# A hash-attention and feed-forward kernel rebuilt around units of 256 queries

## The chip, the cores and the metric

The kernel runs on one core of one Trainium2 chip. Times are device microseconds (us) of that core. The execution that the profiler recorded has a span from the first to the last instruction; the time of a run is a little longer than its span. A "ratio" below is the mean time of one kernel's fast runs over the mean time of the other's fast runs of the same rounds, so it is not the ratio of the medians that stand beside it. A run counts as fast within 1.5% of the fastest run of its kernel in the same rounds; the kernel before varies more than that, so ratios of different rounds are not comparable with one another, and kernels are compared below by their medians. PE is the matmul engine, PEld its weight loads, DVE the vector engine, ACT the engine for exp, POOL the general one, SP the one that issues most DMAs. "The clock" is the granted PE clock that the profile lists, 1.00 being full speed. PSUM is the memory in which the kernels keep the outputs of their matmuls; a bank is here a piece of it of 512 fp32 columns. A row group is one of the four sets of 32 partitions (32i to 32i+31).

## The reference

Four batches, eight heads, 768 positions, head size 64. A query attends to the keys that have the same six-bit hash; the result is normalised over 512 features and goes through a feed-forward of 512 to 2048 to 512 with a residual.

```python
q_bits = (np.einsum('bhsd,dk->bhsk', q, proj) > 0)        # 6 bits; k_bits the same
mask = q_bucket[:, :, :, None] == k_bucket[:, :, None, :]  # bucket: the 6 bits as a number
scores = np.where(mask, q @ k.T / sqrt(64), -1e9)
attn = softmax(scores)                                     # its sum gets + 1e-9
x = (attn @ v), heads side by side -> [4, 768, 512]
xn = (x - mean) / sqrt(var + 1e-6) * g_ln
out = x + maximum(xn @ w_ch1, 0) @ w_ch2
```

Both kernels get the mask from a matmul: the six signs of q and k are extra rows of the contraction, so that a pair with unequal signs gets a score so low that exp makes it nothing.

## The kernel before

For each batch three stages follow one another: a prologue (transposes, hashes), attention, and normalisation with feed-forward.

```python
for b in range(B):
    ...
    for h in range(H):                       # prologue: transposes in fp32
        ...
                        nc.tensor.transpose(tp[:, c, :], src[:, hh * half + c, :], identf)
                    nc.vector.tensor_copy(dstf[:, sl], tp)      # fp32 copy, for the hash
                    nc.scalar.copy(dst[:D, sl], tp)             # bf16 copy, for the scores
    for srcf, dst, mul in ((qTf_b, qprime_b, BIG), (kTf_b, kprime_b, 1.0)):
        for hx in range(HS // 512):          # prologue: hashes, fp32, 6 output rows
            ...
            nc.tensor.matmul(sp, proj_f, srcf[:, sl])
            nc.scalar.sign(dpart, sp)
    for h in range(H):                       # attention
        for qg in range(n_qg):
            for kj in range(n_stile):
                nc.tensor.matmul(sc, kprime[:, ksl], rhs_q)     # 70 rows: 64 and 6 signs
                nc.scalar.activation(expb, sc, AF.Exp, scale=scale, bias=bias_sb)   # 384 columns
                nc.tensor.matmul(avp, v_aug[:, kj, :], expb, ...)   # v is stationary
            ...                              # copy, PE transposes back, division
    ...                                      # normalisation, PE transposes
    for nt in range(n_htile):                # feed-forward, first half; then the second
        ...
```

The softmax here doesn't subtract the row's maximum and nothing guards it: scores larger than these inputs give would overflow.

## Time and profile before

The median was 741.25 us over the first three runs (723.31 to 741.81). In all later rounds this kernel gave times between 713 and 743 us; the shorter runs are those with a higher mean clock (712.96 us at 0.885, 741.52 us at 0.827 in the same rounds); why the clock differs was not examined. The profiled run is one of the short ones, with a span of 714.1 us at clock 0.878.

From the chain of waits in order of time:

| stage, by batch | where in the span (us) | what is busy |
|---|---|---|
| loads and weight casts | 0 to 31 | DMA |
| prologue | 31 to 108, and 60 us in each later batch | PE, on fp32 |
| attention | about 52 us in each batch | ACT |
| normalisation and feed-forward | about 54 us in each batch | PE, on bf16 |

The page of the kernel before, busy tenths in 40 slices of 17.9 us, by engine, with the granted clock under them:

```profile
PE   0089999978997998996997798996998898997897
ACT  0044439974206437994303536995312543997420
PEclk9999999998999556997999855997999755898899
```

ACT is at 9 only where attention runs. PE is near 9 nearly everywhere, but in each of the three later batches the clock falls to 5 or 6 for two or three slices. The table of windows for one piece of attention, one of feed-forward and one of the hashes shows what these are (columns: window; its length; busy us and instruction count of PE, PEld, DVE, ACT, POOL; clock; share of DMA; GB/s):

```profile
110.00:120.00 10.00, 9.80 (x52) 4.93 (x51) 5.28 (x28) 9.88 (x22) 0.00 (x0) 1.00 0.00 0
200.00:215.00 15.00, 13.77 (x64) 5.97 (x64) 3.97 (x7) 1.18 (x3) 0.00 (x0) 1.00 0.27 98
255.00:275.00 20.00, 18.87 (x25) 2.69 (x24) 0.00 (x0) 6.96 (x12) 0.00 (x0) 0.50 0.03 6
```

Attention: ACT is busy for 9.88 of 10 us. Feed-forward: PE alone works, at full clock. Hashes: PE alone works, 18.87 of 20 us, at half clock. The groups of instructions of the same run (line, engine, operation, output and inputs with their shapes, count, then busy us and the mean ns of one, then idle time before them):

```profile
L152 ACT ACTIVATE expb<-sc,bias_sb 128x384 bf16<-128x384 f32 x384 | 182.9, 858 | 0.6
L153 PE MATMUL avp<-expb,vaug_b 128*65 128x384 bf16 x384 | 129.3, 337 | 10.3 <-ACT expb L152 9.0
L133 PE MATMUL spf<-kTf_b,proj_f 64*6 64x512 f32 x96 | 84.0, 1051 | 0.0
L133 PE MATMUL spf<-qTf_b,proj_f 64*6 64x512 f32 x96 | 69.9, 819 | 1.5 <-DVE qTf_b L125 1.5
L206 PE MATMUL hp<-xnT,w_sb 128*128 128x384 bf16 x512 | 94.7, 330 | 3.6 <-ACT xnT L198 3.4
```

The hashes keep PE busy for 84.0 + 69.9 = 154 us to produce 6 rows. Such a line's busy time counts overlapping instructions once, so 384 exps in 182.9 us are 0.476 us each, although one takes 858 ns from start to end.

### The profile page before, as it was taken

How to read it: one execution, taken by the hardware profiler on the slowest of the kernel's cores; microseconds unless marked ns; L12 is line 12 of the kernel's file. 1: busy time of each engine (PE TensorE's matmuls, PEld its weight loads, DVE VectorE, ACT ScalarE, POOL GpSimd, SP SyncE). 2: the span in 40 equal slices, each digit the busy share in tenths (PEclk: the TensorE clock that was granted, in tenths of full speed). 3: DMA queues.
4: the chain of work that ended last, by engine and by line, in shares of the span. 5: the costliest groups of instructions: out<-in, count | busy, mean ns of one | idle time of the engine just before them, and what ended most of it. 6: DMA issues, size and time to landing. Idle time of an engine off the chain costs nothing.

```text
span 714.1 us, 7683 instructions
## 1 busy us (share of the span) xinstructions
PE 611.2 (86%) x2520; PEld 242.2 (34%) x2528; DVE 307.8 (43%) x1028; ACT 359.5 (50%) x728; POOL 19.0 (3%) x44
## 2 busy tenths in 40 slices
PE   0089999978997998996997798996998898997897
PEld 0022214435542212443542212443543221443553
DVE  0444304676325402668424510668423420568431
ACT  0044439974206437994303536995312543997420
POOL 0010000010000000002000000002000000000000
PEclk9999999998999556997999855997999755898899
DMA  8674300012023200003013310002013200000001
GB/s 316 210 135 99 73 17 1 0 42 49 10 82 96 67 11 0 1 2 88 12 59 89 85 23 0 1 2 55 13 45 88 56 1 0 1 2 0 1 15 74
DMA packets 81576, 34.32 MB, mean 48 GB/s; under 512 B 75776, under 2 KB 75776, under 8 KB 81024
## 3 DMA queue, kind: packets, MB, share of 16 engines
q1 hardware_dynamic: 81536, 33.83, 17.7%
q8 instruction: 20, 0.33, 0.2%
q14 instruction: 20, 0.16, 0.1%
HBM read 27.53 MB, written 6.29 MB: 47 GB/s over the span
## 4 chain that ended last, share of the span: by engine, by line
PE 79%; DVE 8%; ACT 7%; DMA 4%; issue 1%; SPq 0%
PE spf L133 21%; PE hp L206 13%; PE avp L153 12%; PE sc L150 10%; PE tp L121 7%; DMA w_f<-in_moe_w_ch_dram 3%; PE avt_p L162 3%; ACT qprime_b L135 2%; ACT kprime_b L126 2%; DVE stats L178 2%; PE xnTp L195 2%; DVE qTf_b L125 1%; DVE xn L191 1%; ACT qprime_b L126 1%; ACT xnT L198 1%
## 5 line engine op out<-in xcount | busy, mean ns | idle before, releaser
L152 ACT ACTIVATE expb<-sc,bias_sb 128x384 bf16<-128x384 f32 x384 | 182.9, 858 | 0.6
L153 PE MATMUL avp<-expb,vaug_b 128*65 128x384 bf16 x384 | 129.3, 337 | 10.3 <-ACT expb L152 9.0
L150 PE MATMUL sc<-qprime_b,kprime_b 70*128 70x384 bf16 x384 | 130.6, 347 | 0.0
L206 PE MATMUL hp<-xnT,w_sb 128*128 128x384 bf16 x512 | 94.7, 330 | 3.6 <-ACT xnT L198 3.4
L158 DVE CAST avs<-avp 65x384 bf16<-65x384 f32 x64 | 35.4, 552 | 130.8 <-PE avp L153 130.8
L135 ACT ACTIVATE qprime_b<-spf 6x512 bf16<-6x512 f32 x48 | 28.2, 588 | 123.9 <-PE spf L133 123.9
L121 PE MATMUL tp<-identf,qnat 128*64 128x128 f32 x192 | 40.4, 343 | 52.7 <-DMA qnat<-in_q_dram 34.5
L133 PE MATMUL spf<-kTf_b,proj_f 64*6 64x512 f32 x96 | 84.0, 1051 | 0.0
L133 PE MATMUL spf<-qTf_b,proj_f 64*6 64x512 f32 x96 | 69.9, 819 | 1.5 <-DVE qTf_b L125 1.5
L125 DVE COPY kTf_b<-tp 64x384 f32<-64x384 f32 x64 | 35.1, 549 | 79.2 <-PE tp L121 79.1
L206 PEld LDWEIGHTS <-w_sb 128*128 128x128 bf16 x512 | 50.0, 98 | 43.1 <-issue 10.7
L211 ACT ACTIVATE hbuf<-hp 128x384 bf16<-128x384 f32 x64 | 31.4, 490 | 57.2 <-PE hp L206 57.2
L213 DVE TENSOR_SCALAR hbuf<-hp 128x384 bf16<-128x384 f32 x64 | 35.7, 558 | 53.4 <-PE hp L206 51.3
L153 PEld LDWEIGHTS <-vaug_b 128*65 128x65 bf16 x384 | 44.2, 116 | 39.2 <-issue 24.4
L150 PEld LDWEIGHTS <-kprime_b 70*128 70x128 bf16 x384 | 38.5, 101 | 55.7 <-issue 46.6
L135 ACT ACTIVATE kprime_b<-spf 6x512 bf16<-6x512 f32 x48 | 28.2, 588 | 56.1 <-PE spf L133 56.1
L218 PEld LDWEIGHTS <-hbuf 128*128 128x128 bf16 x384 | 37.5, 98 | 44.8
L121 PE MATMUL tp<-identf,knat 128*64 128x128 f32 x192 | 44.9, 347 | 7.1 <-ACT qprime_b L126 7.1
L166 DVE CAST avt<-avt_p 128x65 f32<-128x65 bf16 x192 | 37.5, 223 | 22.6 <-PE avt_p L162 17.9
L126 ACT CAST qprime_b<-tp 64x384 bf16<-64x384 f32 x64 | 30.1, 472 | 31.0 <-DVE qTf_b L125 30.6
L121 PEld LDWEIGHTS tp<-identf,knat 128*64 128x64 f32 x192 | 20.0, 131 | 73.3 <-issue 43.2
L125 DVE COPY qTf_b<-tp 64x384 f32<-64x384 f32 x64 | 34.2, 547 | 24.3 <-PE tp L121 24.0
(152 smaller groups left out, 447.6 us busy)
## 6 DMA issues: line engine op xcount, KB each, us to landing
w_f<-in_moe_w_ch_dram SPq DMA_DIRECT2D x2, 4096.0 KB, 19.6
qnat<-in_q_dram SPq DMA_DIRECT2D x32, 192.0 KB, 2.5
knat<-in_k_dram SPq DMA_DIRECT2D x32, 192.0 KB, 2.6
vnat_f<-in_v_dram SPq DMA_DIRECT2D x32, 192.0 KB, 2.9
out_dram<-res SPq DMA_DIRECT2D x24, 256.0 KB, 2.0
gln_sb<-in_moe_g_ln_dram SPq DMA_DIRECT2D x1, 256.0 KB, 4.9
proj_f<-in_proj_dram SPq DMA_DIRECT2D x1, 1.5 KB, 1.9
```

What stands on the lines that cost most here:

```text
L121: nc.tensor.transpose(tp[:, c, :], src[:, hh * half + c, :], identf)
L125: nc.vector.tensor_copy(dstf[:, sl], tp)
L126: nc.scalar.copy(dst[:D, sl], tp)
L133: nc.tensor.matmul(sp, proj_f, srcf[:, sl])
L135: nc.scalar.sign(dpart, sp)
L150: nc.tensor.matmul(sc, kprime[:, ksl], rhs_q)
L152: nc.scalar.activation(expb, sc, AF.Exp, scale=scale, bias=bias_sb)
L153: nc.tensor.matmul(avp, v_aug[:, kj, :], expb, start=(kj == 0), stop=(kj == n_stile - 1),)
L166: nc.vector.tensor_copy(avt, avt_p)
L206: nc.tensor.matmul(hp, w1_sb[:, dt, nt * P : (nt + 1) * P], xnT[:, dt, msl], start=(dt == 0), stop=(dt == n_dtile - 1),)
L213: nc.vector.tensor_scalar_max(hbuf[:, nt, msl], hp, 0.0)
L218: nc.tensor.matmul(o2, hbuf[:, nt, si * P : (si + 1) * P], w2_sb[:, nt, :], start=(nt == 0), stop=(nt == n_htile - 1),)
```

## The change

The kernel is written anew, with a schedule by hand: every piece of work gets a key, a step number, and all pieces are issued in the order of their keys. A unit is 256 queries of all eight heads, and takes six steps; a step treats four heads, two key tiles and 256 queries. The intent: fewer and wider instructions, PE transposes removed, and feed-forward of earlier units issued between the steps of later ones, so that PE always has work while ACT does the exps. The core of the new kernel (cuts marked):

```diff
-            for kj in range(n_stile):
-                nc.tensor.matmul(sc, kprime[:, ksl], rhs_q)
-                nc.scalar.activation(expb, sc, AF.Exp, scale=scale, bias=bias_sb)
-                nc.tensor.matmul(avp, v_aug[:, kj, :], expb, ...)
+    def scores(s):                       # 24 matmuls; head i uses rows 32i to 32i+31, bank i
+        sc[s] = psum.tile([P, 4, 512], F32, name=f"sc{s}", tag="sc")     # one buffer, 4 banks
+        for kk in range(2):
+            for rep in range(3):         # 6 sign rows, then two halves of 32 features
+                for i in range(4):
+                    r = slice(32 * i, 32 * i + (NB if rep == 0 else 32))
+                    ...
+                    nc.tensor.matmul(sc[s][:, i, 256 * kk : 256 * kk + 256], lh, rh, ...)
+    def exps(s):                         # one instruction of 2048 columns
+        nc.scalar.activation(E[s], sc[s], AF.Exp, scale=EXP_SCALE, bias=bias_sb)
+    def av(s):                           # exp is stationary, v streams: 16 matmuls of 65 columns
+        for kk in range(2):
+            for i in range(4):
+                for qt in range(2):
+                    nc.tensor.matmul(acc[u, g][:, qt, (D + 1) * i : (D + 1) * (i + 1)],
+                        E[s][:, i, 256 * kk + P * qt : ...], vaug[u // 3][:, 4 * g + i, 2 * kp + kk], ...)
 ...
+    def turn(dst, src, j, kj0, n):       # q and k: 32x32 transposes on DVE
+        nc.vector.transpose(d[:, j, kj0 : kj0 + n], s[:, j, kj0 : kj0 + n])
+    def flip(u):                         # normalised rows: transposes by DMA
+        nc.sync.dma_start_transpose(out=xnT[u][:, qt], in_=xc[u][:, qt])
 ...
+    def ff1(u, p, bank):                 # a chunk: 8 matmuls of 256 columns, then a relu
+        f1 = psum.tile([P, 2, 256], F32, name=f"f1_{u}{p}", tag=bank)    # one bank
+        ...
+        nc.vector.tensor_scalar_max(hb[u][:, 2 * p : 2 * p + 2], f1, 0.0)
+    def ff2(u, t, qtr, bank):            # a chunk: 4 matmuls of 512 columns
 ...
+    for s in range(NS):                  # 72 steps
+        at(s, scores, s)
+        at(s + 0.05, exps, s)
+        at(s + 1.07, av, s)
+    def ff(fn, *a):                      # the feed-forward chunks, 2.67 in a step, from step 8.5 on
+        key = 8.5 + 0.375 * chunk[0]
+        chunk[0] += 1
+        at(key, fn, *a)
```

Hashes of the first batch are small fp32 matmuls at the start; those of later batches use four column groups of 32, during the steps of the batch before, and 16 small DMAs bring their bits to the right rows. The casts of q, k and v are POOL's, the layer norm's scale is folded into the first weight, and `vsum` with a factor of 2^-100 gives rows without any matching key the mean of v that the reference gives them.

## The prediction

> **What bounds the kernel now.** Stage by stage (table of windows, chain of waits), the kernel does three things for each of four batches, almost one after the other: a prologue of fp32 transposes and fp32 hash matmuls (about 77, 60, 58 and 61 us), attention (about 52 us each) and layer norm with feed-forward (about 54 us each), after 31 us of weight loads and casts. Each stage has another limit. The prologue is bound by PE: in the groups of instructions the hash matmuls (64x512 fp32, only 6 output rows) are busy for 154 us and are 21% of the chain; the fp32 transposes are busy for 85 us. While the hash matmuls run alone the granted clock falls to 0.50. Attention is bound by ACT: in the timeline an exp of 128x384 starts every 0.47 us, with ACT 100% busy and PE waiting. Feed-forward is bound by PE[...]: 16 matmuls of 384 columns take 2.74 us (171 ns each), 16 of 512 take 3.45 us (216 ns each), while ACT and DVE are mostly idle.
>
> **What the change does.** It puts the three stages on top of each other, so that the sum of three limits becomes about the PE's sum. Removed from PE: the transposes of q and k (to DVE's 32x32 transposes), of the attention output (exp is now stationary, so queries come out on partitions) and of the normalised rows (to DMA). Hashes become 12 small full-width matmul pairs in batch 0 and six column-tiled groups after. Exps become 72 of 2048 columns.
>
> **Cost, per step (72 steps).**
> - ACT: the measured 0.47 us for 384 columns[...].
> - PE scores: 24 row-tiled matmuls of 256 columns.[...]
> - PE values: 16 pairs of a 128-column weight load and 65 streamed columns[...].
> - PE feed-forward: the same 393k columns; 2.67 chunks of 0.86 to 0.96 us: 2.43.
> - Fallback rows and hashes[...]
> Sum 4.9 us. Scores have a single PSUM buffer, so exp, scores, exp is a serial chain of about 3.4 us; it is hidden under 4.9 us and binds only in the first 8.5 steps, which have no feed-forward.
>
> **Total.** Start about 10, 8.5 steps at 3.5 (30), 63.5 steps at 4.9 (310), a tail of 26 chunks (24), last store 4: span about 378; times were somewhat above the span before (714 against 723 to 742), so about 387 us.
>
> **What would show it.** PE over 90% busy with clock near 1.0 from about 40 us on; no fp32 transposes on PE; step period (start to start of exps) 4.9 us in the middle, 3.5 at the beginning; ACT about 35 to 40%; DVE about 40 to 45%; ff matmuls at 110 to 125 and 216 ns; a PE-only tail of 20 to 27 us.
>
> **What would make it wrong.** Row tiles that do not overlap (scores 2.6 us a step: +100 us).[...] The single banks of the feed-forward: relu from PSUM (0.56 us for 384 columns now, so about 0.7 for 512) behind other DVE work could stall PE.[...] Slower than before would need the serial chain above 9 us a step.

The sum of a step came to 4.9 us. Of its terms only feed-forward still stands, with 2.43 us, the author's estimate from the 216 ns and 171 ns measured for 512 and 384 columns. The other 2.5 us are the cut terms for scores with changes of tiling, for values, and for fallback rows and hashes. The chain of about 3.4 us, and with it the 3.5 us of the first steps, has cut terms in it too, for exp and scores; so the total of 387 us is partly a sum of terms that can no longer be read here. The 2.6 us a step for row tiles that do not overlap are an estimate of 24 matmuls at about 110 ns, near what 171 ns for 384 columns gives for 256; the +100 us beside them are taken against the cut term.

## The result, and the profile after

The kernel after takes 365.48 us (median of 4 runs, 365.04 to 365.71), the kernel before 732.28 us in the runs counted here (716.42 to 741.81); the ratio is 0.507, with an interval of 0.503 to 0.512. The result is correct, and all four runs are fast ones. Of the kernel before, only the two shorter runs (723.31 and 716.42 us) are within 1.5% of its fastest, which is the main reason why the ratio is not 365.48 / 732.28. The measured time is 22 us below the predicted one.

The page of the kernel after, in 40 slices of 9.1 us:

```profile
PE   8674457989988989989989989898889899897993
ACT  2344204662453554445246445533535455442000
PEclk9989555899999999999999999999999999999899
```

The alternation of before is gone: from the eighth slice to the thirty-sixth PE stands at 8 to 9, and ACT mostly at 4 to 6. Before that, in the fifth to seventh slice, PE is busy for 4 to 7 tenths and the clock falls to 0.5. The table of windows, for the start (up to the tenth exp), the middle, and the tail (after the last value matmul):

```profile
0.00:67.80 67.80, 45.05 (x461) 28.45 (x462) 27.95 (x68) 20.78 (x14) 24.75 (x36) 0.75 0.76 185
67.80:331.30 263.50, 242.83 (x3688) 167.09 (x3744) 142.53 (x283) 123.91 (x63) 74.51 (x68) 1.00 0.34 81
331.30:363.90 32.60, 24.82 (x142) 14.22 (x142) 12.85 (x23) 0.00 (x0) 1.22 (x2) 0.94 0.21 52
```

In the middle PE is busy for 242.83 of 263.5 us, 92%, at clock 1.00. The groups of instructions:

```profile
L189 ACT ACTIVATE E<-sc,bias_sb 128x2048 bf16<-128x2048 f32 x72 | 141.6, 1967 | 173.9 <-PE sc L182 173.9
L248 PE MATMUL f<-xnT,w_sb 128*128 128x256 bf16 x768 | 99.7, 274 | 16.3 <-DVE hb L252 13.8 <-DMA xnT<-xc 2.3
L182 PE MATMUL sc<-qb,kb 32*128 32x256 bf16 x1152 | 54.2, 275 | 0.0
L206 PE MATMUL acc<-vaug,E 128*128 128x65 bf16 x1152 | 49.5, 198 | 0.0
```

Exps fell from 182.9 to 141.6 us of ACT. The value matmuls fell from 129.3 to 49.5 us of PE. First-half feed-forward stayed where it was, 94.7 against 99.7 us, because its columns are the same (512 x 384 and 768 x 256). One step in the timeline (start us, length us, engine, line, operation; merged over neighbours; weight loads, DVE, DMA and the middle rounds of the scores are left out):

```profile
181.23 0.29 PE L182 MATMUL sc<-G 6*128 6x256 bf16 x4
181.68 0.39 PE L182 MATMUL sc<-qb,kb 32*128 32x256 bf16 x8
182.00 0.66 PE L206 MATMUL acc<-vaug,E 128*128 128x65 bf16 x16
182.18 1.97 ACT L189 ACTIVATE E<-sc,bias_sb 128x2048 bf16<-128x2048 f32 x1 [2.14 <-PE sc L182]
182.50 1.04 PE L248 MATMUL f<-xnT,w_sb 128*128 128x256 bf16 x8
183.38 1.03 PE L258 MATMUL f<-w_sb,hb 128*128 128x512 bf16 x3
184.34 0.29 PE L182 MATMUL sc<-G 6*128 6x256 bf16 x4
```

Scores start at 181.23, the value matmuls of the step before at 182.00, two chunks of feed-forward follow at 182.50 and 183.38 while the exp runs from 182.18 to 184.15, and the next scores start at 184.34. All 24 score matmuls together take 0.77 us up to the first value matmul. From the starts of single matmuls in the trace: a round of four row tiles comes every 0.11 us; value matmuls follow each other every 31 ns in the mean; first-half matmuls every 109 ns, second-half ones every 216 ns (medians).

The exps of the thirteenth and the sixty-seventh step start 54 x 4.27 us apart. So a step in the middle takes 4.27 us, where 4.9 had been predicted.

### The profile page after: what moved, and what is told of

Its sections match the earlier page's. It is cut to its first block, busy times and chain, and to the rows that moved or that the text cites. A ratio compares the mean times of both kernels' runs of the same rounds, so it can differ in the third digit from the quotient of the medians.

```text
span 363.9 us, 9678 instructions
## 1 busy us (share of the span) xinstructions
PE 312.7 (86%) x4281; PEld 209.8 (58%) x4344; DVE 183.3 (50%) x373; ACT 144.7 (40%) x76; POOL 100.5 (28%) x106
## 4 chain that ended last, share of the span: by engine, by line
PE 66%; DVE 15%; SPq 5%; DMA 4%; issue 3%; ACT 3%; POOL 1%; ACTq 0%; DVEq 0%; POOLq 0%
PE f L248 19%; PE f L258 18%; PE sc L182 11%; PE acc L206 8%; PE hf L301 4%; SPq L133 4%; DVE hb L252 3%; ACT E L189 3%; PE hp L123 2%; DVE xc L231 2%; DMA w1f<-in_moe_w_ch_dram 2%; DMA xnT<-xc 2%; PE warm L354 2%; DVE x L221 2%; DVE st L223 1%
## 5 line engine op out<-in xcount | busy, mean ns | idle before, releaser
L189 ACT ACTIVATE E<-sc,bias_sb 128x2048 bf16<-128x2048 f32 x72 | 141.6, 1967 | 173.9 <-PE sc L182 173.9
L248 PE MATMUL f<-xnT,w_sb 128*128 128x256 bf16 x768 | 99.7, 274 | 16.3 <-DVE hb L252 13.8
L252 DVE TENSOR_SCALAR hb<-f 128x512 bf16<-128x512 f32 x96 | 65.6, 683 | 52.7 <-PE f L248 51.4
L258 PE MATMUL f<-w_sb,hb 128*128 128x512 bf16 x321 | 86.9, 385 | 3.5
L182 PE MATMUL sc<-qb,kb 32*128 32x256 bf16 x1152 | 54.2, 275 | 0.0
L258 PEld LDWEIGHTS <-hb 128*128 128x128 bf16 x384 | 35.2, 99 | 30.5 <-issue 3.2
L206 PEld LDWEIGHTS <-E 128*128 128x128 bf16 x1152 | 43.1, 100 | 11.4 <-issue 10.5
L206 PE MATMUL acc<-vaug,E 128*128 128x65 bf16 x1152 | 49.5, 198 | 0.0
L182 PE MATMUL sc<-G 6*128 6x256 bf16 x576 | 41.9, 280 | 4.0 <-ACT E L189 3.9
L182 PEld LDWEIGHTS <-kb 32*128 32x128 bf16 x1152 | 30.8, 96 | 2.0
```

Of the source, the lines that this page charges most:

```text
L182: nc.tensor.matmul(sc[s][:, i, 256 * kk : 256 * kk + 256], lh, rh, start=(rep == 0), stop=(rep == 2), skip_group_check=True,)
L189: nc.scalar.activation(E[s], sc[s], AF.Exp, scale=EXP_SCALE, bias=bias_sb)
L206: nc.tensor.matmul(acc[u, g][:, qt, (D + 1) * i : (D + 1) * (i + 1)], E[s][:, i, 256 * kk + P * qt : 256 * kk + P * qt + P], vaug[u // 3][ ...
L248: nc.tensor.matmul(f1[:, n].rearrange("p (t x) -> p t x", t=2), w1_sb[:, dt, P * nt : P * nt + P], xnT[u][:, :, dt], start=(dt == 0), stop ...
L252: nc.vector.tensor_scalar_max(hb[u][:, 2 * p : 2 * p + 2], f1, 0.0)
L258: nc.tensor.matmul(f2[u, t], hb[u][:, nt, P * t : P * t + P], w2_sb[:, nt], start=(nt == 0), stop=(nt == NNT - 1),)
```

## The experiments

Times are medians; unless said otherwise the kernel changed is the one after, 365.48 us, and the result stays correct. The runs are in four groups, on four chips, each beside the kernel before, whose median was 742.23, 741.52, 741.73 and 742.04 us. The kernel after itself was not run again beside them, so how much of a small difference is the chip's is not known. One of them, whose order of issue turned out not to matter, came within 0.4% of it.

### Score matmuls head by head

```diff
-            for rep in range(3):
-                for i in range(4):
+            for i in range(4):
+                for rep in range(3):
```

> Edit: in the scores, the three partial products of one head are issued one after the other, then the next head; the same 24 matmuls a step, but neighbours now share their 32 rows of the array instead of using the other 96. Theory (four row tiles run at once; that is why the scores took 0.77 us of a step instead of four times as much): neighbours cannot overlap, a matmul of 256 columns takes about 110 to 130 ns, scores 2.6 to 3.1 us, step 4.2 -> 6.2 us, in all 365 -> about 490 to 520 us. Rival (the order of issue does not matter, the array or its queue finds the free row groups by itself, or the matmuls are simply short): within 2% of 365 us.

It took 366.71 us (365.95 to 367.18; ratio to the kernel before 0.494). My theory's number was missed by more than 120 us, and the rival's was met. But the trace shows that this run did not test the theory. The timeline of one step of this kernel:

```profile
182.35 0.31 PE L182 MATMUL sc<-G 6*128 6x256 bf16 x4
182.47 0.41 PE L182 MATMUL sc<-qb,kb 32*128 32x256 bf16 x8
182.69 0.30 PE L182 MATMUL sc<-G 6*128 6x256 bf16 x4
182.81 0.41 PE L182 MATMUL sc<-qb,kb 32*128 32x256 bf16 x8
```

The program's order is one matmul of six sign rows (`G`), two of 32 rows (`kb`), then the next head. What ran is four of `G` first, then eight of `kb`, as in the kernel after: the single starts in the trace are 182.352, .362, .372 and .382 us for the four of six rows, and only 182.472 for the first of 32 rows, which is second in the program. In 53 of 54 middle steps the order is the same. That it was PE and not the build that changed the order is argued from the distances: within a round of four they are 3 ns in the kernel after and 10 ns here (medians), which fits the program: there the sign matmul of the next head comes three instructions later, not one. By this trace, then, three matmuls of other row groups started ahead of an older one of the first row group, 90 ns before it in the step shown; what held the older one back was not shown. The same overlap came about, and the question stayed open.

### All heads on one row group, and on two

```diff
-                    r = slice(32 * i, 32 * i + (NB if rep == 0 else 32))
+                    r = slice(0, NB if rep == 0 else 32)                                    # one
+                    r = slice(32 * (i % 2), 32 * (i % 2) + (NB if rep == 0 else 32))        # two
```

Both give wrong results (heads get the scores of other heads); counts, shapes and banks are unchanged.

> Edit of the kernel after: all four heads of a group take their operands from the first 32 rows (wrong result on purpose: every head gets the scores of the first), so the 24 score matmuls of a step share one row group and no order can overlap them; everything else is the same. The earlier run with another order did not test this: its trace shows that PE started matmuls of other row groups ahead of their turn. Theory (four row groups really run at once): scores take 24 x about 110 ns = 2.6 us instead of 0.67 us, a step grows from 4.2 to about 6.1 us, time about 500 us. Rival (matmuls of 6 and 32 rows are short anyway, row groups give nothing): within 2% of 365 us.

> The same with two row groups (heads 0 and 2 on one, 1 and 3 on the other; wrong result on purpose). Theory: scores 12 x 110 ns = 1.3 us, a step about 4.85 us, time about 410 us, so a third of what one group costs. Rival: as before, within 2% of 365 us.

One group took 548.21 us (542.63 to 557.11), two took 406.81 us (403.96 to 411.63); one run of each is slow, and without it the medians are 545.85 and 404.79 us. The theory holds, and the rival falls: from first to last start (medians over the middle steps), the 24 matmuls of a step take 2.53 us with one group, 1.22 us with two, 0.575 us with four. The trace with two groups is of a slow run, 411.63 us, but the middle of it, where this was read, ran at clock 1.00. Two groups met the expected number within 2%. One group took 46 us more than expected. The windows of its trace show the clock:

```profile
20.00:60.00 40.00, 36.98 (x193) 24.23 (x192) 11.17 (x26) 8.39 (x5) 10.20 (x11) 0.50 0.67 153
250.00:300.00 50.00, 48.34 (x436) 33.77 (x436) 17.58 (x34) 13.78 (x7) 13.79 (x12) 0.86 0.09 20
```

PE is busy for 92% and 97% of these stretches, yet the clock is 0.50 in the first and 0.86 in the second. With four groups it is 1.00 in the middle at 92% busy. A step took 6.68 us in the mean instead of the 6.1 expected at full clock; the median is 6.15. What lowered the clock was not isolated.

### Feed-forward in blocks

```diff
-        key = 8.5 + 0.375 * chunk[0]
+        key = 8.5 + 6.0 * (chunk[0] // 16) + 0.0001 * (chunk[0] % 16)
```

> Edit: the 16 feed-forward chunks of a query unit stand in one block, instead of 2.67 after each attention step; same instructions. Theory (without chunks a step is bound by the serial chain exp 1.97 us, wait, scores 0.8 us, about 3.0 us, because the scores have one PSUM buffer; the chunks fill PE in that time): a unit takes 5 x 3.0 + about 17 = 32 us against 25.3 us, in all about 425 to 445 us. Rival (PE's sum bounds the kernel whatever the order): within 2% of 365 us.

It took 473.41 us (471.68 to 474.40; ratio 0.638): 108 us more, with exactly the same instructions. The rival falls. The theory has the direction, but the result lies 28 us above its range. Two steps of the blocked kernel, at full and at lower clock, and the granted clock in 40 slices:

```profile
256.83 1.97 ACT L189 ACTIVATE E<-sc,bias_sb 128x2048 bf16<-128x2048 f32 x1 [1.00 <-PE sc L182]
259.80 1.97 ACT L189 ACTIVATE E<-sc,bias_sb 128x2048 bf16<-128x2048 f32 x1 [1.00 <-PE sc L182]
263.40 1.97 ACT L189 ACTIVATE E<-sc,bias_sb 128x2048 bf16<-128x2048 f32 x1 [1.63 <-PE sc L182]
266.99 1.97 ACT L189 ACTIVATE E<-sc,bias_sb 128x2048 bf16<-128x2048 f32 x1 [1.63 <-PE sc L182]
PEclk9886569598779589598679689598679589588599
```

A step without chunks takes 2.97 us as long as the clock is full: 1.97 us of exp and the 1.00 us at the end of the line, in which ACT waits for the next scores. That is the serial chain, as predicted. But some 8 us after a block, with PE idle for half of each step, steps become 3.59 us: the merged pieces of the scores take 0.40 and 0.66 us there where they took 0.29 and 0.40 before, and the granted clock of the slice from 258.4 to 270.2 us is 0.6. The span's mean clock is 0.788 against 0.948. Over the nine units in the middle, a unit takes 35.1 us in the mean where 32 was expected: 17.6 us for the interval with the block, and 3.5 us for each of the five steps without chunks where 3.0 had been assumed. So most of the miss lies in these steps.

### Feed-forward in blocks, and matmuls that nobody reads

```diff
+    def fill(s):
+        wp = psum.tile([P, 512], F32, name=f"fill{s}", tag="f1")
+        for _ in range(5):
+            nc.tensor.matmul(wp, warm[:, 0:P], warm, start=True, stop=True)
+    for s in range(12, NS - 1):
+        if s % 6 != 1:
+            at(s + 1.08, fill, s)
```

> The kernel with feed-forward in blocks (473 us) plus five matmuls of 512 columns on constants, whose result nobody reads, after the value matmuls of every attention step without a block, from step 12 on: about 50 us of extra work for PE. In the blocked kernel a step takes 2.95 us as long as the clock is 1.0 and 3.6 us once it has fallen to 0.5, which it does some 7 us after a block. Theory (part of what blocking costs is clock, lost because PE is idle for half of an attention step): the fill fits in the wait for exp, clock stays near 1.0, steps stay at about 3.0 us and the first chunks of a block no longer run at half speed; time falls to about 440 us in spite of the extra work. Rival (the clock follows from something else, or hardly matters): time stays at 473 us or grows.

It took 456.66 us (453.75 to 457.94; ratio 0.616), 17 us less than the blocked kernel with some 50 us more work for PE, with a mean clock of 0.927 instead of 0.788 in the profiled runs, which is the clearest sign that clock was lost there. Its granted clock:

```profile
PEclk9895559589989999999989999999989999999799
```

After the start it stays at 0.9 to 1.0 in nearly every slice, and the exps of most steps without chunks start 2.97 us apart (4.24 us in some). The expected 440 us were missed: in the same nine units the steps without chunks went from 3.5 to 3.1 us in the mean, as the theory says, but the interval with the block stayed at 17.8 us, and the average step went only from 5.87 to 5.62 us. Of the 108 us that blocking costs, then, at least 17 us came back with the clock; the rest is the chain and waits inside the blocks, which were not told apart further.

### One exp for each head

```diff
-        nc.scalar.activation(E[s], sc[s], AF.Exp, scale=EXP_SCALE, bias=bias_sb)
+        for i in range(4):
+            nc.scalar.activation(E[s][:, i], sc[s][:, i], AF.Exp, scale=EXP_SCALE, bias=bias_sb)
```

> Edit: the exp of a step is four instructions of 512 columns, one for each head, instead of one of 2048. Theory (ACT is off the path in the middle of the kernel, so the wide exp saves ACT time but hardly any kernel time): ACT busy 142 -> about 165 to 175 us, time within 2%, perhaps 2 to 5 us longer from the first nine steps, which have no chunks and hang on the chain. Rival (the saving in ACT, 41 us against the kernel before, is on the path): 25 to 40 us longer.

It took 369.88 us (369.04 to 369.94; ratio 0.498): 4 us more, with ACT's exps at 174.2 us instead of 141.6. So the wide exp saved 33 us of ACT and 3 to 4 us of time (3 against the run with scores head by head, 366.71 us, on the same chip); the rival falls. A step in the middle went from 4.27 to 4.33 us. The line of the exps in this kernel:

```profile
L190 ACT ACTIVATE E<-sc,bias_sb 128x512 bf16<-128x512 f32 x288 | 174.2, 688 | 148.1 <-PE sc L182 148.1
```

### v as stationary again

```diff
-                for qt in range(2):
-                    nc.tensor.matmul(acc[u, g][:, qt, 65 columns of head i], E[s][:, i, 128 queries], vaug[...])
+                nc.tensor.matmul(acc[u, g][: D + 1, 256 queries of head i], vaug[...], E[s][:, i, 256 queries])
+    def evict(u, g):                 # before the division: copy, then eight PE transposes
+        nc.vector.tensor_copy(avs[u, g][: D + 1], acc[u, g][: D + 1])
+        ...
+                nc.tensor.transpose(a[:, qt, i, : D + 1], avs[u, g][...], ident[: D + 1, : D + 1])
```

> Edit: in the value matmuls v is stationary again (65 columns) and exp streams (8 matmuls of 256 columns a step for 16 of 65), so each half unit needs a copy from PSUM and eight PE transposes before the division; the result stays correct. Theory (streaming exp costs its columns, 8 x about 110 ns = 0.9 us a step against 0.55 us for the 16 pairs with exp as stationary, and the transposes and copies come on top, some of them as waits at a bank that feed-forward also uses): plus 0.35 us a step = 25 us, plus 1 to 1.5 us a half unit = 25 to 35 us; in all 400 to 430 us. Rival (loading 128x128 weights for only 65 columns is no gain[...]): 375 to 390 us, from the transposes alone.

It took 416.76 us (416.36 to 417.50; ratio 0.562): 51 us more, in the theory's range, and outside the rival's. A step in the middle takes 5.03 us. Eight value matmuls of 256 columns follow each other every 109 ns, 0.87 us a step against 0.50, which is 0.37 x 72 = 27 us. The rest of the 51 us, about 24 us, was not isolated, but the trace accounts for it roughly: 5 us for the matmuls of the fallback rows, which the turned product makes four of 256 columns instead of two of 260 (24 half units, 0.22 us each), 6 us for PE's transposes (192, 30 ns apart), and the rest waits. These transposes (their line is 229 in this kernel) wait 23.1 us, mostly for a bank that feed-forward uses, while the 13.8 us that first-half feed-forward waited for relus in the kernel after are gone:

```profile
L229 PE MATMUL avt<-ident,avs 65*128 65x65 bf16 x192 | 9.7, 193 | 23.1 <-DVE hb L265 21.8 <-DVE avs L218 1.3
```

### The kernel before with bf16 hashes

```diff
-        qTf_b = head_pool.tile([D, HS], F32, tag="qTf_b", bufs=1)      # and kTf_b
+        qTf_b = head_pool.tile([D, HS], BF16, tag="qTf_b", bufs=1)
-                nc.tensor.matmul(sp, proj_f, srcf[:, sl])
+                nc.tensor.matmul(sp, proj_h, srcf[:, sl])              # proj_h: proj as bf16
```

> Edit of the kernel BEFORE: q and k for the hash and the projection are bf16[...] (wrong result in a few buckets, on purpose: the comparison will fail). Theory (the prologue is bound by PE's fp32 hash matmuls, 21% of the chain): [...]time down by 80 to 115 us, to about 615 to 650 us. Rival (the prologue is bound by its copies, signs and loads just as much, so the time moves elsewhere): less than 40 us gained.

It took 628.89 us (627.39 to 630.25) against 741.52 us of the unchanged kernel before in the same rounds (712.96 to 743.11), so about 113 us less by the medians, with a relative error of 0.124, wrong. But ten of the eleven runs of the kernel before count as slow; fast against fast (712.96 us) the gain is 84 us. The busy time of the hash matmuls fell from 154 to 52.5 us. How far the author expected it to fall rested on no trace or run of this case and is cut; the expected gain of 80 to 115 us is an estimate made from it:

```profile
L135 PE MATMUL spf<-kTf_b,proj_h 64*6 64x512 bf16 x48 | 26.3, 591 | 3.6 <-ACT kprime_b L137 3.3
L135 PE MATMUL spf<-qTf_b,proj_h 64*6 64x512 bf16 x48 | 26.2, 546 | 0.6 <-DVE qTf_b L127 0.6
```

The theory holds, at the lower end of its range: most of the 101 us of PE became time, so the prologue of the kernel before was bound mainly by these matmuls. The rival's shift came only in part: the fp32 transposes of q and k kept PE busy for 100.4 us here instead of 85.3. It also bounds what the rebuilding gained there: with a hash that costs little, the kernel before would still have needed about 629 us, and the other 263 us to the kernel after come from elsewhere. The removal of the fp32 transposes was not tested by itself.

### The order of the first nine steps

In the kernel after the timeline shows DVE at a standstill in the start:

```profile
45.96 0.48 DVE L316 TENSOR_SCALAR w_sb<-w1f,g_sb 128x512 bf16<-128x512 f32 x1 [5.23 <-DMA w1f<-in_moe_w_ch_dram]
46.36 0.76 DVE L288 STREAM_TRANSPOSE T<-X 128x256 f32<-128x256 f32 x2
46.85 2.08 PE L301 MATMUL hf<-T,pfull 128*128 128x256 f32 x4 [5.78 <-DVE T L288]
```

A cast of the first weight waits 5.23 us for its load. Behind it in DVE's program stands a transpose of q, which starts at 46.36 us; for it a hash waits (5.78 us, to 46.85 us), which stands in PE's program ahead of the next scores. Two more such pairs of transpose and hash, each behind a cast, follow at 49.70 and 53.04 us before the scores come at 55.53 us. The sixth and the seventh exp start 16.9 us apart here. The edit moves keys, and gives the last pieces of q, whose hashes are needed from steps 12 and 15 on, the buffers of the k pieces; the sum of v on POOL for the second four heads moves too (key 3.4 to 2.45):

```diff
-    at(0.25, load_w1, 1)
+    at(3.45, load_w1, 1)                       # and the loads of the last q pieces ahead of it
-    at(5.6, first, 0, 0, 2, ...)               # a hash of q that is needed from step 12 on
+    at(7.2, first, 0, 0, 2, ...)
-            at(3.6 + 0.8 * n + 0.2 * dt, cast_w1, n, dt)
+            at(5.35 + 1.0 * n + 0.05 * dt, cast_w1, n, dt)
 ...
```

> Edit of the kernel after: in the first nine steps, casts of w1, which wait for their load, stand later in DVE's order, and hashes of q that are needed only from step 6 and 12 on stand later too; loads in that order. Theory (the first nine steps take 51 us instead of about 27 because DVE, in order, stands at a w1 cast that waits for its load while transposes that the scores wait for stand behind it): step 9 starts at 48 to 55 us instead of 65, time 350 to 357 us. Rival (the loads themselves bound the start, DMA is 70 to 110% busy in it): within 1% of 365 us.

It took 349.53 us (349.03 to 350.06), 16 us less. The tenth exp starts at 52.9 us instead of 67.8 us, and the window from 40 to 50 us reads, in the kernel after and in this one:

```profile
40.00:50.00 10.00, 3.15 (x24) 2.08 (x20) 2.93 (x8) 1.97 (x1) 1.49 (x1) 0.50 0.87 282
40.00:50.00 10.00, 7.01 (x100) 4.89 (x96) 7.92 (x23) 4.75 (x3) 3.11 (x3) 0.66 1.03 203
```

The time is just under the theory's range, the start of step 9 inside it: DVE's wait for the load fell from 5.2 to 0.6 us. Up to 2.5 us may be the moved sum of v, for which PE waited 4.2 us before and 1.7 us here. The rival falls as a full explanation; with DMA at 1.03 here, loads may be what bounds the rest of the start.

### Some relus on ACT

```diff
+        if fn is ff1 and 0.1 <= key % 3 < 1.0:      # chunks right behind a division or centering
+            a = a + (True,)                          # on_act
...
+        if on_act:
+            nc.scalar.activation(hb[u][:, 2 * p : 2 * p + 2], f1, AF.Relu)
```

> Edit of the kernel after: relus of chunks that come right after a division or a centering (about a third of them) run on ACT, which is 60% idle. Theory (the 14 us that PE waits for relus come from relus standing behind the division and the centering in DVE's order): that wait falls from 14 to under 5 us, time down by 5 to 10 us. Rival (the single bank itself is the limit: any evacuation of about 0.7 us plus its latency leaves the gap): within 1%.

It took 355.47 us (353.06 to 357.98), 10 us less. The list of waits has PE's wait for relus in the kernel after; in this kernel no such line is among those listed, and what PE waits for in first-half feed-forward is the DMA transposes:

```profile
PE f L248 <- DVE hb L252: 13.8, 11, 2.1
PE f L248 <- DMA xnT<-xc: 2.3, 2, 1.3
```

```profile
PE f L248 <- DMA xnT<-xc: 7.2, 5, 2.3
```

So 13.8 us of waiting for relus went and 4.9 us of waiting for the transposes came; the difference, 8.9 us, is close to the 10 us of time. It was the order of DVE's work, not the single bank as such.

### Both, and both with two more

> Both edits of the two kernels before in one. Theory: they are in different stretches, so the gains add up: 342 to 352 us. Rival: no better than the better of the two.

Both edits together took 340.67 us (339.37 to 344.06), 25 us less than the kernel after, so the gains of 16 and 10 us add up. This version is the best, 7% below the kernel after.

The last kernel adds two edits to that one:

```diff
-            nc.sync.dma_start_transpose(out=xnT[u][:, qt], in_=xc[u][:, qt])
+            nc.scalar.dma_start_transpose(out=xnT[u][:, qt], in_=xc[u][:, qt])
+        if u == NU - 1 and p % 2:                    # last unit: a second bank for the chunks
+            f1 = psum.tile([P, 2, 512], F32, ..., tag="acc")[:, 0].rearrange(...)
```

> The kernel with both edits (start order and relus on ACT, 341 us) plus two more: the DMA transposes of the normalised rows are issued from ACT's queue, because on SP's queue they stand behind 16 small moves of hash bits[...], and the last unit's first feed-forward matmuls alternate between two banks. Theory: the 6.6 us that PE waits for the transposes mostly go, the tail loses 2 to 3 us: 332 to 338 us. Rival (issuing from ACT delays exps and relus by as much): 340 us or more.

It took 396.55 us (394.41 to 402.03; ratio 0.535), 56 us more than without them. The rival is right, and by far more than I had thought possible. The timeline at a transpose (ACTq is ACT's own queue of instructions) shows the reason:

```profile
219.39 2.73 ACTq L238 DMA_TRANSPOSE xnT<-xc  x2
222.17 0.60 ACT L256 ACTIVATE hb<-f 128x512 bf16<-128x512 f32 x1 [3.71 <-issue]
222.81 1.22 PE L251 MATMUL f<-xnT,w_sb 128*128 128x256 bf16 x8 [3.33 <-ACT hb L256]
```

Issuing two transposes holds ACT's queue from 219.39 to 222.1 us (two took 2.5 us on SP's queue in the kernel after), and already before that the queue stands, since the transposes wait for the centering; ACT is idle for 3.71 us ahead of the relu. A relu and an exp stand behind them, and PE waits 3.33 us for that relu. The list of waits gives PE 39.6 us in 11 such waits, and the mean clock falls to 0.917. Between the thirteenth and the sixty-seventh exp this kernel takes 268.9 us, the one without the two edits 223.8 us: 45 of the 56 us arise there, where the second edit has no part, since the last unit's first feed-forward matmuls all come after the last exp. The second edit cannot be judged from this run. As for the moves of hash bits that the expectation names: in the kernel after each takes SP's queue 0.72 us in the median, and seven of them, 5.36 us from 182.77 us on, stand just ahead of two transposes at 188.25 us.

## Why the prediction was right

The measured 365.48 us lies 22 us, 6%, below the predicted 387 us. Point by point:

**The idea: three stages with different limits become one stage bound by PE.** Right. In the middle PE is 92% busy at clock 1.00, and ACT 124 of 263.5 us. Putting the same instructions in blocks again costs 108 us. The wide exp by itself is worth 3 to 4 us only, as it should be if ACT is off the path.

**The sum of a step** was 4.9 us; it is 4.27 us. The terms, measured:

| term | predicted us | measured us |
|---|---|---|
| scores, 24 matmuls | cut | 0.68: first to last start 0.575, and 0.109 for the last, the distance of the 256-column matmuls in feed-forward |
| changes of tiling | cut | 0.19: the matmul after a change starts 96 ns later than the usual distance, 89 ns on the way back |
| values, 16 pairs | cut | 0.50: 16 x 31 ns |
| fallback rows and hashes | cut | 0.19: two matmuls of 110 ns in three steps; six hashes of about 1.4 us in 72 steps |
| (the cut terms together) | 2.5 | 1.56 |
| feed-forward, 2.67 chunks | 2.43 | 2.34: 8 x 111 ns or 4 x 216 ns, half of each |
| sum | 4.9 | 3.9 |
| waits | none | 0.37: the rest to 4.27 |

The largest error lies in the cut terms, 2.5 us of the sum, which measure 1.56 us. A pair of a weight load of 128 columns and 65 streamed columns costs 31 ns in the trace, and turning the product round again cost 51 us. The opposite error is that the sum had no waits: relus that stand behind a division or a centering on DVE, of which the prediction spoke only as a risk, cost about 10 us. What the rest of the 0.37 us is was not told apart. An exp of 2048 columns takes 1.97 us, off the path; the estimate for it is cut.

**The start** was to take 10 us and 8.5 steps of 3.5 us, 40 us to the ninth or tenth step; the tenth exp starts at 67.8 us. This is the step of the prediction that failed, by some 25 us: it took the serial chain of exp and scores as the only limit of the first steps. The chain itself took less than predicted (2.97 us at full clock against 3.4), but in four of the first nine intervals between exps it does not bind: these are 7.8, 4.7, 7.4 and 16.9 us long, together 25 us more than four chains. What binds there is the order of work in DVE's and PE's queues, behind loads; the run with moved keys shows that for 15 us of the 28 by which the tenth exp came late.

**The tail** was to take 24 us and 4 for the store; it takes 32.6 us, of which PE is busy for 24.8.

So the total came out close partly by luck: a middle that was 46 us shorter than predicted (263.5 us against 310) met a start and a tail that were about 32 us longer.

**Row tiles.** The largest risk named, "row tiles that do not overlap, +100 us", did not come: a round of four starts every 0.11 us, as single matmuls of 256 columns do in feed-forward (109 ns). For the 24 matmuls of a step the traces show 2.64 us on one group, 1.33 on two and 0.68 on four (first to last start, plus 0.109 for the last), 3.9 times less on four than on one. Without the overlap it would have cost about 180 us (545.85 against 365.48 us) and not 100, at a lower clock (0.828 in the profiled run, against 0.948).

**What did not show as listed:** "PE over 90% busy with clock near 1.0 from about 40 us on" holds only from about 68 us on; ACT at 40%, DVE at 50%, matmuls at 109 to 111 and 216 ns were near what was listed; "no fp32 transposes on PE" holds.

## What to carry to other kernels

When stages with different limits follow one another, issue them into each other at the grain of a few us: here the same instructions took 108 us more in blocks, with the mean clock at 0.788 instead of 0.948, and matmuls that nobody reads, put into PE's pauses, brought 17 us of them back. Look at what stands in the queue of an engine ahead of the urgent work and what that waits for; a new order in the start and relus moved to ACT, without any new work, gained 25 of 365 us, and a DMA issue put into ACT's queue (with a small edit of the tail) lost 56. A sum of costs by engine came within 15% of a step in the middle of this kernel (4.9 us against 4.27); the start needs a look at loads and queue order of its own.
